# Gated linear attention and a SoLU layer on one core: block transposes placed by four SBUF-to-SBUF DMAs, attention values made as [d, tokens], and the variance of z summed by ScalarE

## The chip, the cores and the metric

The kernel runs on one core of a Trainium2 chip. The metric is device time in microseconds (us) of one execution. Five engines work side by side, each through its own list of instructions in order: PE (TensorE: matmuls, with weight loads shown apart as PEld), DVE (VectorE), ACT (ScalarE), POOL (GpSimd) and SP (SyncE, which here only issues DMAs). SP and ACT can both issue DMAs; in the profile these issues stand as SPq and ACTq.

## The reference, cut to what matters

```python
# attention: q, k, v, a_re, a_im are [B=4, H=8, S=768, D=48]
for t in range(S):                                   # state S_re, S_im: [B, H, D, D]
    new_re = ar * S_re - ai * S_im                   # (ar, ai): the gate of step t, |a| clamped to 0.999
    new_im = ar * S_im + ai * S_re
    S_re, S_im = new_re + k[t] (x) v[t], new_im
    y[:, :, t] = q[t] @ S_re
x = y as [B*S, H*D]                                  # 3072 tokens x 384
# SoLU layer
h = x @ w_in                                         # 384 -> 1024
z = h * softmax(h)
ln = (z - mean(z)) / sqrt(var(z) + 1e-6) * g_ln
out = ln @ w_out                                     # 1024 -> 384
```

Everything is float32 on the chip.

## The kernel before, in words

The sequence is cut into 6 pieces of 128 tokens; with 4 batches that gives 24 chunks `c = 0..23` (`ti, b = divmod(c, 4)`). Two neighbouring chunks form a group `g` (12 of them), for which the gates are prepared together (`prep_steps`). Inside a chunk the recurrence is written as decayed k and q of 96 numbers per head (cosine and sine halves), so that attention is a masked 128x128 product of q and k, plus a product of q with the state of 96x384 that all earlier tokens left (`state[b]`).

The steps of a chunk that the change touches, in the order in which one chunk goes through them:

- `k2`, `q2` (L880, DVE) write the decayed k and q into `f_kq`, tokens on partitions. They are needed with the 96 numbers on partitions and the tokens along the row. `kqb` (L888, DVE) transposes them in blocks of 32x32 into `f_kb`; `kqt0..2` (L896) then bring the blocks to their places in `f_kqT` by 12 DMAs of 32 rows, 6 issued by SP and 6 by ACT. (Chunks 0 and 1 use PE transposes instead.)
- `score0/1` (L937, PE): k times q, in tiles of 32 columns. `mask0` (L941, DVE) masks them into `f_att`, whose rows are key tokens and whose columns are query tokens.
- `values` (L954 and L957, PE): `f_att` as weights, 32 query tokens at a time, times v (48 columns a head), plus `f_kqT` as weights times the state. The result `f_y` has tokens on partitions. `f_vr` is a copy of v of the odd heads with its 32-row blocks in reverse order, since the scores of odd heads lie so.
- `x` (L962, ACT) copies `f_y` from PSUM; `turn_x` (L993, PE) transposes it by three 128x128 products with the identity; `turned_x` (L997, ACT) copies that into `f_xT`.
- `carry` (L970, PE) and `add` (L975 on, DVE) bring the state forward. The PSUM tile of `carry` is the one of `f_y`.
- `up0/1` (L1003, PE), `exp0` (L1008, ACT, with the sum of exponentials), `solu0` (L1011, DVE: h times exp, into `f_z`).
- `blocks` (L1028, DVE) transposes `f_z` in 32x32 blocks into `f_zb`; `away` (L1034) writes them to DRAM by 4 DMAs; `back` (L1039) reads them from DRAM by one DMA as `f_zT`, with the 1024 features on partitions. (Chunks 0, 1, 2 and 23 use PE transposes, `zt` and `zT`.)
- `norm` (L1052 on): mean and variance of z by two `bn_stats` and a `bn_aggr` on DVE, then four small POOL instructions to `f_rs`.
- `down0/1` (L1064, PE), `scale` (L1069, ACT, times `f_rs`), `store` (SP).

The order on every engine is written out by hand: the lists START, EVEN, ODD and END name steps with a chunk number beside each (in EVEN and ODD relative to the chunk `n` of the turn, with `g1`, `g2` for groups), and each step appends its instructions to its engines. EVEN and ODD alternate for n = 2..19, so a period of the loop is a pair of chunks. Each DMA, on SP or ACT, takes the next of 8 semaphores in rotation and waits until the DMA that had it before is done.

Of the kernel before, what the change touches and what calls it, by code (L numbers as in the profile page):

```python
# [19 lines left out]
P = 128  # L20
# [506 lines left out]
phase0:1 load_k:2 last:1 phase1:1 ks1:1 mean:2 qs1:1 mask0:1 convert:12 nearest0:1 nearest1:1 raised:11 part0:1
part1:1 again:0 values:1 clamp:2 cos:1 mean:3 load_vr:3 ends:1 again:1 sin:1 x:1 exp:1 turn_x:1 mean:4
convert:11 again:4 inverse:2 zt0:0 k2:2 mean:5 q2:2 kqb:2 turned_x:1 zT0:0 load_ai:3 kqt0:2 kqt1:2 k2:3 kqt2:2
mean:6 ratio:2 mean:7 tangent:2 q2:3 square:2 secant:2 turn_ends:1 zt1:0 centre:0 fourth:2 centre:7 load_q:2  # L530
up0:1 centre:5 centre:4 up1:1 zT1:0 score0:2 size:2 eps:2 again:2 kqb:3 exp0:1 load_ar:3 tot:1 kqt0:3 centre:1
# [12 lines left out]
square:g2 secant:g2 fourth:g2 ks1:g1 ends:g1 up0:0 load_k:g2 k2:2 q2:2 back:-1 score0:1 zT0:-1 score1:1
load_ai:g3 zt1:-1 turn_ends:g1 size:g2 load_ar:g3 scale:-2 eps:g2 kqb:2 add:0 lnm:g2 tot:g1 mask0:1 zT1:-1 up1:0
kqt0:2 norm:-1 kqt2:2 exp0:0 total1:g2 grow1:g2 inspect:1 total0:g2 grow0:g2 store:-2 decay1:g2 solu0:0 ks0:g2
decay0:g2 store:-3 trig:g2 angle:g2 kqt1:2 blocks:0 on:g2 down0:-1 away:0 down1:-1
# [22 lines left out]
def whole(ctx, tc, flag, q, k, v, a_re, a_im, moe_w_in, moe_w_out, moe_g_ln, out):  # L570
# [634 lines left out]
```

## Time and profile before

| | us |
|---|---|
| median of 3 runs (lowest to highest) | 489.3 (488.15 to 493.79) |
| the profiled execution, its own time | 487.12 |
| the span of its trace, first to last instruction | 484.5 |
| PE busy | 418.7 (86%) |
| DVE busy | 385.8 (80%) |
| ACT busy | 266.6 (55%) |
| POOL busy | 40.8 (8%) |

Some 2.6 us of the profiled execution lie outside the span of its trace. A busy share says how long an engine had work in flight; an engine that is 86% busy can still be the one that everybody waits for in a stage, and what a stage waits for is read from the idle time just ahead of its instructions. The rows that matter are shown in the prediction. PE counts each float32 product as two instructions.

### The profile page before, as it was taken

How to read it: one execution, taken by the hardware profiler on the slowest of the kernel's cores; microseconds unless marked ns; L12 is line 12 of the kernel's file. 1: busy time of each engine (PE TensorE's matmuls, PEld its weight loads, DVE VectorE, ACT ScalarE, POOL GpSimd, SP SyncE). 2: the span in 40 equal slices, each digit the busy share in tenths (PEclk: the TensorE clock that was granted, in tenths of full speed). 3: DMA queues.
4: the chain of work that ended last, by engine and by line, in shares of the span. 5: the costliest groups of instructions: out<-in, count | busy, mean ns of one | idle time of the engine just before them, and what ended most of it. 6: DMA issues, size and time to landing. Idle time of an engine off the chain costs nothing.

```text
span 484.5 us, 14751 instructions
## 1 busy us (share of the span) xinstructions
PE 418.7 (86%) x6244; PEld 282.6 (58%) x6244; DVE 385.8 (80%) x555; ACT 266.6 (55%) x417; POOL 40.8 (8%) x110
## 2 busy tenths in 40 slices
PE   0257977999999988988989998998998997999994
PEld 0035544555676665566666676576675674577762
DVE  5889999798999889789789899689799788482430
ACT  4989967666654743753735654654753743522120
POOL 0000000000001101100110101101001001010010
PEclk9999987999999999999989999999999998999998
DMA  9887957948868769769669759659659758255321
GB/s 246 187 199 216 220 136 178 253 108 175 226 147 200 193 149 212 183 145 210 170 164 225 208 135 216 169 125 222 180 134 214 181 136 224 62 151 145 97 68 41
DMA packets 173419, 82.99 MB, mean 171 GB/s; under 512 B 145312, under 2 KB 158624, under 8 KB 173344
## 3 DMA queue, kind: packets, MB, share of 16 engines
q1 hardware_dynamic: 166864, 72.97, 62.8%
q10 hardware_dynamic: 6480, 8.99, 7.1%
q8 instruction: 51, 0.84, 0.8%
q14 instruction: 24, 0.20, 0.1%
HBM read 49.35 MB, written 15.20 MB: 133 GB/s over the span
## 4 chain that ended last, share of the span: by engine, by line
PE 38%; DMA 19%; DVE 17%; SPq 15%; issue 5%; ACT 4%; ACTq 0%; DVEq 0%
PE f_o L1064 17%; PE f_h L1003 9%; SPq L896 7%; DMA f_zT<-f_zd 6%; DMA f_kqT<-f_kb 5%; SPq L1034 4%; DMA f_zd<-f_zb 3%; DVE f_kb L888 3%; DVE f_kq L880 3%; DMA f_q<-in_q_dram 3%; PE f_score L937 2%; PE f_phase L830 2%; PE f_y L954 2%; DVE f_zb L1028 2%; SPq L648 2%
## 5 line engine op out<-in xcount | busy, mean ns | idle before, releaser
L1064 PE MATMUL f_o<-f_w_out,f_zT 128*128 128x384 f32 x384 | 140.9, 517 | 17.6 <-DMA f_zT<-f_zd 17.1
L1064 PEld LDWEIGHTS f_o<-f_w_out,f_zT 128*128 128x128 f32 x384 | 111.4, 298 | 38.3 <-ACT f_ar L783 12.9
L1003 PE MATMUL f_h<-f_w_in,f_xT 128*128 128x512 f32 x288 | 131.3, 600 | 0.6 <-issue 0.6
L1003 PEld LDWEIGHTS f_h<-f_w_in,f_xT 128*128 128x128 f32 x288 | 52.9, 190 | 56.6 <-issue 53.9
L1008 ACT ACTIVATE f_z<-f_h 128x1024 f32<-128x1024 f32 x24 | 24.5, 1023 | 54.8 <-PE f_h L1003 36.4
L888 DVE STREAM_TRANSPOSE f_kb<-f_kq 128x1536 f32<-128x1536 f32 x22 | 39.1, 1777 | 12.0 <-DMA f_kqT<-f_kb 11.6
L962 ACT COPY f_xn<-f_y 128x384 f32<-128x384 f32 x24 | 11.5, 478 | 64.1 <-PE f_y L957 48.3
L1011 DVE TENSOR_TENSOR f_z<-f_h,f_z 128x1024 f32<-128x1024 f32 x24 | 29.0, 1209 | 19.7 <-ACT f_z L1008 19.7
L1028 DVE STREAM_TRANSPOSE f_zb<-f_z 128x1024 f32<-128x1024 f32 x20 | 41.0, 2052 | 0.4
L937 PEld LDWEIGHTS f_score<-f_kqT 96*32 96x32 f32 x1536 | 29.9, 112 | 17.8 <-issue 16.6
L937 PE MATMUL f_score<-f_kqT 96*32 96x128 f32 (+3 forms) x1536 | 33.6, 239 | 6.6 <-issue 4.3
L776 PE MATMUL f_L<-f_lr,f_mats 128*128 128x384 f32 x48 | 20.4, 553 | 20.8 <-DVE f_lr L771 20.8
L941 DVE TENSOR_TENSOR f_att<-f_score,f_mats 128x1024 f32<-128x1024 f32 x24 | 29.1, 1211 | 6.8 <-PE f_score L937 6.7
L837 DVE SCALAR_TENSOR_TENSOR f_f<-f_f,f_phase 128x384 f32<-128x384 f32 x24 | 13.1, 549 | 26.0 <-ACT f_f L833 26.0
L957 PE MATMUL f_y<-f_state,f_kqT 96*32 96x48 f32 x1280 | 30.8, 206 | 0.0
L1052 DVE BATCH_NORM_STATS2 f_bs<-f_z 128x6 f32<-128x512 f32 x48 | 30.4, 671 | 0.0
L997 ACT COPY f_xT<-f_xt 128x384 f32<-128x384 f32 x24 | 11.4, 476 | 31.4 <-PE f_xt L993 22.6
L957 PEld LDWEIGHTS f_y<-f_state,f_kqT 96*32 96x32 f32 x1280 | 28.4, 110 | 0.2
L776 PEld LDWEIGHTS f_L<-f_lr,f_mats 128*128 128x128 f32 x48 | 9.9, 212 | 29.6 <-DVE f_lr L771 21.4
L954 PE MATMUL f_y<-f_v,f_att 128*32 128x48 f32 x768 | 25.6, 209 | 0.7 <-DVE f_att L941 0.7
L1057 POOL TENSOR_TENSOR f_s<-f_s,f_mv 128x1 f32<-128x1 f32 x24 | 5.0, 208 | 247.1 <-DVE f_mv L1053 247.1
L954 PEld LDWEIGHTS f_y<-f_v,f_att 128*32 128x32 f32 x768 | 16.4, 109 | 14.8 <-issue 11.1
(98 smaller groups left out, 662.1 us busy)
## 6 DMA issues: line engine op xcount, KB each, us to landing
f_zd<-f_zb SPq DMA_DIRECT2D x80, 128.0 KB, 2.7
f_zT<-f_zd SPq DMA_DIRECT2D x20, 512.0 KB, 3.9
f_kqT<-f_kb ACTq DMA_DIRECT2D x132, 64.0 KB, 3.7
f_kqT<-f_kb SPq DMA_DIRECT2D x132, 64.0 KB, 2.0
f_raw<-in_moe_w_out_dram SPq DMA_DIRECT2D x16, 384.0 KB, 4.2
f_raw<-in_moe_w_in_dram SPq DMA_DIRECT2D x12, 512.0 KB, 4.2
f_ar<-in_a_re_dram SPq DMA_DIRECT2D x12, 384.0 KB, 7.9
f_ai<-in_a_im_dram SPq DMA_DIRECT2D x12, 384.0 KB, 5.3
```

Source lines behind the costliest of these rows:

```text
L776: nc.tensor.matmul(out=ps, lhsT=tri, rhs=st["lr"][:, i * DM:(i + 1) * DM], start=True, stop=True)
L888: nc.vector.transpose(out=t, in_=T["kq", c].rearrange("p n h (j f) -> p j (n h) f", f=32))
L896: eng.dma_start(out=T["kqT", c][j * 32:(j + 1) * 32, r], in_=st["kb"][r * 32:(r + 1) * 32, j])
L937: nc.tensor.matmul(out=scores[r0:r0 + 32, x, r:], lhsT=QK[:, r // 32, x], rhs=QK[:, r // 32:, H + x], start=True, stop=True)
L941: nc.vector.tensor_tensor(out=st["att"].rearrange("p (i u) t -> p i u t", u=2), in0=scores.rearrange("p (i u) t -> p i u t", u=2), in1=mat ...
L954: nc.tensor.matmul(out=y[r:r + 32, hs], lhsT=st["att"][:, x, r:r + 32], rhs=rhs, start=True, stop=(ti == 0))
L957: nc.tensor.matmul(out=y[r:r + 32, hs], lhsT=T["kqT", c][:, r // 32, H + x], rhs=state[b][:, hs], start=False, stop=True)
L1003: nc.tensor.matmul(out=st["h"][:, half * 512:(half + 1) * 512], lhsT=st["xT"][:, c * P:(c + 1) * P], rhs=w_in[:, c, half * 512:(half + 1) ...
L1011: nc.vector.tensor_tensor(out=st["z"], in0=st["h"], in1=st["z"], op=OP.mult)
L1028: nc.vector.transpose(out=st["zb"].rearrange("p s t c -> p s c t"), in_=st["z"].rearrange("p (c s f) -> p s c f", s=4, f=32))
L1052: nc.vector.bn_stats(out=bs[:, i], in_=z[:, i * 512:(i + 1) * 512])
L1064: nc.tensor.matmul(out=st["o"], lhsT=st["zT"][:, c] if n in SHORT else st["zT"][:, :, c], rhs=w_out[:, c], start=(c == 0), stop=(c == KF - 1))
```

## The change

Four things change, all in the steps above; the rest of the order stays.

1. `kqb` reads the columns of k and q at a step of 3 elements (12 bytes), so that block element f of block j is feature 3f+j. The 32 rows of a strip and its 3 blocks then follow each other in the order of the 96 features, and one DMA per strip (4 for a chunk, all issued by SP) fills all 96 partitions. `kqt1` and `kqt2` go.
2. `blocks` reads z at a step of 4 elements (16 bytes) in the same manner; `away` takes the blocks from `f_zb` to `f_zT` directly, by 4 DMAs from SBUF to SBUF. `back` and the DRAM tile go.
3. `values` now has v and the state as weights (32 or 16 features) and `f_att` and `f_kqT` as moving data (128 tokens), so that `f_y` comes out with features on partitions; `turned_x` copies it straight into `f_xT`. `x` and `turn_x` go. So that features fill whole strips of 32, `f_vr` and the state get zero columns (odd heads begin 16 columns in), which POOL clears once at the start.
4. `solu0` also sums z; `centred` (POOL) makes minus the mean of it; `spread` (ACT) squares z minus the mean in place, with a sum; `norm` is four POOL instructions on that sum. `bn_stats` and `bn_aggr` go.

```diff
-again:1 values:0 phase0:g1 phase1:g1 qs1:g1 norm:-1 x:0 nearest0:g1 inspect:-1 carry:0 nearest1:g1 qs0:g1
+again:1 values:0 phase0:g1 phase1:g1 qs1:g1 norm:-1 turned_x:0 nearest0:g1 inspect:-1 carry:0 nearest1:g1 qs0:g1
...
-    state = [const.tile([D2, DM], FP, name=f"f_state{b}") for b in range(B)]
+    state = [const.tile([D2, H // 2, P], FP, name=f"f_state{b}") for b in range(B)]
+    odds = [const.tile([P, 2, H // 2, 64], FP, name=f"f_vr{i}") for i in range(3)]
...
-            nc.vector.transpose(out=t, in_=T["kq", c].rearrange("p n h (j f) -> p j (n h) f", f=32))
+            nc.vector.transpose(out=t, in_=T["kq", c].rearrange("p n h (f j) -> p j (n h) f", j=3))
...
-            for r in ((0, 1), (2,), (3,))[i]:
-                for j in range(3):
-                    eng = KQ_ENGINES[i]
-                    eng.dma_start(out=T["kqT", c][j * 32:(j + 1) * 32, r], in_=st["kb"][r * 32:(r + 1) * 32, j])
+            for r in range(4):
+                nc.sync.dma_start(out=T["kqT", c][:, r].rearrange("p x t -> p (x t)"),
+                                  in_=st["kb"][r * 32:(r + 1) * 32].rearrange("p j x t -> p j (x t)"))
...
-            for x in range(H):
-                hs = slice(x * D, (x + 1) * D)
-                rhs = T["vr", g][:, own, x // 2] if x % 2 else V[:, hs]
-                for r in range(0, P, 32):
-                    nc.tensor.matmul(out=y[r:r + 32, hs], lhsT=st["att"][:, x, r:r + 32], rhs=rhs, start=True,
-                                     stop=(ti == 0))
-                for r in range(0, P if ti > 0 else 0, 32):
-                    nc.tensor.matmul(out=y[r:r + 32, hs], lhsT=T["kqT", c][:, r // 32, H + x],
-                                     rhs=state[b][:, hs], start=False, stop=True)
+            queues = [[], [], [], []]
+            for p in range(DM // 32):
+                i, part = divmod(p, 3)
+                todo = []
+                for u in ((0,), (1, 0), (1,))[part]:
+                    x, w = 2 * i + u, 32 if part != 1 or u else 16
+                    o, s0 = 32 * (part - u), 32 * part + 16 * u
+                    vals = T["vr", g][:, own, i, o:o + w] if u else V[:, x * D + o:x * D + o + w]
+                    todo.append((w, vals, st["att"][:, x]))
+                    if ti > 0:
+                        todo.append((w, state[b][:, i, s0:s0 + w], T["kqT", c][:, :, H + x]))
+                for k, (w, lhsT, rhs) in enumerate(todo):
+                    r, c0 = p % 4 * 32, p // 4 * P
+                    queues[p % 4].append(dict(out=y[r:r + w, c0:c0 + P], lhsT=lhsT, rhs=rhs, start=(k == 0),
+                                              stop=(k == len(todo) - 1)))
+            for todo in zip(*queues):
+                for product in todo:
+                    nc.tensor.matmul(**product)
...
-            nc.scalar.copy(out=st["xT"], in_=st["xt"])
+            nc.scalar.copy(out=st["xT"], in_=T["y", n])
...
-            nc.vector.tensor_tensor(out=st["z"], in0=st["h"], in1=st["z"], op=OP.mult)
+            nc.vector.scalar_tensor_tensor(out=st["z"], in0=st["h"], scalar=1.0, in1=st["z"], op0=OP.mult, op1=OP.mult,
+                                           accum_out=st["sum"][:, 0:1])
...
-                                in_=st["z"].rearrange("p (c s f) -> p s c f", s=4, f=32))
+                                in_=st["z"].rearrange("p (c f s) -> p s c f", s=4, f=32))
...
-                nc.sync.dma_start(out=st["zd"][:, :, r].rearrange("s f x -> f s x"),
-                                  in_=st["zb"][r * 32:(r + 1) * 32].rearrange("p s t c -> p s (t c)"))
-        def back():
-            nc.sync.dma_start(out=st["zT"].rearrange("p t c -> p (t c)"),
-                              in_=st["zd"].rearrange("s f r x -> (s f) (r x)"))
+                nc.sync.dma_start(out=st["zT"][:, r].rearrange("p t c -> p (t c)"),
+                                  in_=st["zb"][r * 32:(r + 1) * 32].rearrange("p s t c -> p s (t c)"))
+        def centred():
+            nc.gpsimd.tensor_scalar(out=st["less"], in0=st["sum"][:, 0:1], scalar1=-1.0 / FF, scalar2=None, op0=OP.mult)
+        def spread():
+            nc.scalar.activation(out=st["z"], in_=st["z"], func=AF.Square, bias=st["less"], accum_out=st["sum"][:, 1:2])
...
-                nc.vector.bn_stats(out=bs[:, i], in_=z[:, i * 512:(i + 1) * 512])
-            nc.vector.bn_aggr(out=mv, in_=bs)
...
+    for t in odds + state:
+        nc.gpsimd.memset(t, 0.0)
```

What the list of SP looks like in the loop, from the load of `f_vr` in EVEN to the second `f_kqT` and the stores in ODD; before:

```order
L658 DMA f_vr<-in_v_dram 32x8x48 x4
L648 DMA f_v<-in_v_dram 128x16x48
L896 DMA f_kqT<-f_kb 32x512 x6
L1034 DMA f_zd<-f_zb 32x4x256 x4
L648 DMA f_k<-in_k_dram 128x16x48
L1039 DMA f_zT<-f_zd 128x1024
L648 DMA f_ai<-in_a_im_dram 128x16x48
L648 DMA f_ar<-in_a_re_dram 128x16x48
L896 DMA f_kqT<-f_kb 32x512 x6
L1074 DMA out_dram<-f_ot 128x384 x2
L1034 DMA f_zd<-f_zb 32x4x256 x4
```

and the same stretch of SP's list in the changed kernel:

```order
L659 DMA f_vr_128<-in_v_dram 32x8x48 x4
L649 DMA f_v<-in_v_dram 128x16x48
L895 DMA f_kqT<-f_kb 96x1x512 x4
L1043 DMA f_zT<-f_zb 128x1x256 x4
L649 DMA f_k<-in_k_dram 128x16x48
L649 DMA f_ai<-in_a_im_dram 128x16x48
L649 DMA f_ar<-in_a_re_dram 128x16x48
L895 DMA f_kqT<-f_kb 96x1x512 x4
L1078 DMA out_dram<-f_ot 128x384 x2
L1043 DMA f_zT<-f_zb 128x1x256 x4
```

The blocks of z go to `f_zT` at the place where they went to DRAM, the second transfer is gone, and 6 issues of `f_kqT` have become 4.

ACT's list from the exponential of the even chunk to the last step ahead of the odd chunk's one (lines 754 to 768 prepare the gates of a later group, `f_ar`, `f_u` and `f_x` are their tiles, and `f_ot` is the scaled output of an earlier chunk), before:

```order
L1008 ACTIVATE f_z,f_sums<-f_h 128x1024
L896 DMA f_kqT<-f_kb 32x512 x3
L962 COPY f_xn<-f_y 128x384
L896 DMA f_kqT<-f_kb 32x512 x3
L997 COPY f_xT<-f_xt 128x384
L754 ACTIVATE f_ar<-f_x_2394 128x768
L757 ACTIVATE f_u<-f_ar,f_bias 128x768
L760 ACTIVATE f_ai,f_seen<-f_ar 128x768
L1069 ACTIVATE f_ot<-f_o,f_rs 128x384
L767 ACTIVATE f_u<-f_lr,f_bias 128x768
L768 ACTIVATE f_u<-f_u,f_bias 128x768
L896 DMA f_kqT<-f_kb 32x512 x3
```

and in the changed kernel:

```order
L1014 ACTIVATE f_z,f_sums<-f_h 128x1024
L1003 COPY f_xT<-f_y 128x384
L755 ACTIVATE f_ar<-f_x_2036 128x768
L758 ACTIVATE f_u<-f_ar,f_bias 128x768
L761 ACTIVATE f_ai,f_seen<-f_ar 128x768
L1054 ACTIVATE f_z,f_sum<-f_z,f_less 128x1024
L1073 ACTIVATE f_ot<-f_o,f_rs 128x384
L768 ACTIVATE f_u<-f_lr,f_bias 128x768
L769 ACTIVATE f_u<-f_u,f_bias 128x768
```

ACT's DMA issues and the copy of `f_y` have left the list, and `spread` (L1054) of the even chunk stands ahead of the scaling of an output. The other `spread` of the pair, of the odd chunk, stands in this stretch of ACT's list, ahead of the copy of `f_xT`:

```order
L817 ACTIVATE f_x_2036<-f_x_2036 128x768
L1054 ACTIVATE f_z,f_sum<-f_z,f_less 128x1024
L1003 COPY f_xT<-f_y 128x384
L834 ACTIVATE f_f<-f_phase,f_bias 128x384 x2
```

Ahead of the copy there stood, before, three DMA issues (L896) and the copy of `f_y` (L962).

More of the change, by code (lines that the diff above doesn't have):

```diff
@@ L527 @@
[L527 to L531, printed above, removed]
@@ L539 @@
-sin:g1 exp:g1 mask0:1 inverse:g2 up0:0 up1:0 back:-1 load_vr:g1 exp0:0 k2:2 q2:2 kqb:2 load_v:g2 values:1 kqt0:2
-ratio:g2 down0:-1 kqt2:2 solu0:0 zt0:0 x:1 turn_x:1 blocks:0 carry:1 down1:-1 kqt1:2 tangent:g2 turned_x:1
-away:0
+again:1 values:0 phase0:g1 phase1:g1 qs1:g1 norm:-1 turned_x:0 nearest0:g1 inspect:-1 carry:0 nearest1:g1 qs0:g1
+part0:g1 add:0 load_q:g2 score1:1 last:g1 again:8 scale:-2 part1:g1 score0:1 cos:g1 clamp:g2 sin:g1 exp:g1
+mask0:1 inverse:g2 up0:0 up1:0 load_vr:g1 exp0:0 k2:2 q2:2 kqb:2 load_v:g2 values:1 kqt0:2 ratio:g2 down0:-1
@@ L542 @@
+solu0:0 zt0:0 turned_x:1 blocks:0 carry:1 down1:-1 tangent:g2 away:0
 """
 ODD = """
[L544 to L547, printed above, removed]
+square:g2 secant:g2 fourth:g2 ks1:g1 ends:g1 up0:0 load_k:g2 k2:2 q2:2 score0:1 zT0:-1 score1:1 load_ai:g3
@@ L559 @@
+store:22 scale:23 store:23
 """
@@ L917, in turn_steps @@
             own["kqb"] = blocked
-            own.update({f"kqt{i}": partial(turned, i) for i in range(3)})
+            own["kqt0"] = turned
         return own
@@ L1080, in ffn_steps @@
         else:
-            own.update(blocks=blocks, away=away, back=back)
+            own.update(blocks=blocks, away=away)
         for half in range(2):
```

97 lines of the change are left out of this document (47 added, 50 removed).

## The prediction

> **What bounds the kernel now.** The head of the page and the busy time of three stretches say where PE stands still: the start-up (0 to 80 us), the loop with the first turns of its end (80 to 440), and the last 45 us. The last row below is one pair of chunks of the loop.
>
> ```profile
> span 484.5 us, 14751 instructions
> 0.00:80.00 80.00, 45.58 (x522) 26.77 (x523) 67.68 (x120) 63.02 (x97) 1.66 (x8) 0.97 0.81 201
> 80.00:440.00 360.00, 335.82 (x5387) 228.57 (x5388) 303.67 (x408) 196.02 (x305) 35.56 (x90) 0.98 0.74 176
> 440.00:485.00 45.00, 37.30 (x355) 27.25 (x341) 14.49 (x28) 7.58 (x16) 3.54 (x12) 0.96 0.27 82
> 325.00:361.20 36.20, 33.32 (x553) 23.47 (x552) 30.84 (x42) 20.14 (x32) 3.65 (x9) 1.00 0.76 176
> ```
>
> Columns: stretch, length, then PE, PEld, DVE, ACT and POOL busy, the granted clock, DMA's share. In the loop PE works 335.82 of 360 us, so 24.2 us is all that a better order could give there; a pair takes 36.2 us, of which PE works 33.3, DVE 30.8, ACT 20.1. What PE waits for in that stretch (from the waits of PE; total, times, longest):
>
> ```profile
> PE f_o L1064 <- DMA f_zT<-f_zd: 17.1, 11, 2.7
> PE f_score L937 <- issue: 3.5, 5, 1.1
> PE f_score L937 <- DMA f_kqT<-f_kb: 2.3, 3, 1.0
> ```
>
> So 17.1 of the 24.2 us is the way of z through DRAM. The chain shows that way inside the pair, start and length:
>
> ```profile
> 318.52 2.07 DVE f_zb L1028
> ...
> 326.42 0.45 SPq L1034
> 326.91 2.70 DMA f_zd<-f_zb
> ...
> 329.62 4.66 DMA f_zT<-f_zd
> ...
> 334.42 5.53 PE f_o L1064 x16
> ```
>
> The blocks are ready at 320.6, the last write is issued at 326.4, lands at 329.6, the read lands at 334.3. SP's own list tells why issuing is late (same place one pair later), and ACT's list that it suffers too:
>
> ```profile
> 347.57 3.89 SPq L658 DMA_DIRECT2D f_vr<-in_v_dram  x4
> 355.46 0.39 SPq L648 DMA_DIRECT2D f_v<-in_v_dram  x1
> 356.05 4.68 SPq L896 DMA_DIRECT2D f_kqT<-f_kb  x6
> ```
> ```profile
> 352.12 2.44 ACTq L896 DMA_DIRECT2D f_kqT<-f_kb  x2
> 354.61 0.48 ACT L962 COPY f_xn<-f_y 128x384 f32<-128x384 f32 x1 [2.52 <-DMA f_kqT<-f_kb]
> 356.53 0.48 ACT L997 COPY f_xT<-f_xt 128x384 f32<-128x384 f32 x1 [1.45 <-DMA f_kqT<-f_kb]
> ```
>
> SP stands from 351.5 to 355.5 ahead of a load because the semaphores go round over SP's and ACT's DMAs, and ACT's were issued only at 352 and later. PE is thus the engine that sets the pair, with DVE close behind and the DMA queues making the holes.
>
> **DMAs.** Per pair the 24 transfers of `f_kqT`, 12 on SP and 12 on ACT, become 8 on SP, and the 2 reads of z go; at 4.68 us for six in the row above, SP gains 3 us of issuing and ACT some 8. The bytes of z are moved once, not twice.
>
> ```profile
> f_zd<-f_zb SPq DMA_DIRECT2D x80, 128.0 KB, 2.7
> f_zT<-f_zd SPq DMA_DIRECT2D x20, 512.0 KB, 3.9
> f_kqT<-f_kb SPq DMA_DIRECT2D x132, 64.0 KB, 2.0
> ```
>
> ```profile
> 334.42 5.53 PE L1064 MATMUL f_o<-f_w_out,f_zT 128*128 128x384 f32 x16 [1.87 <-DMA f_zT<-f_zd]
> ```
>
> The new z transfer I price like the write to DRAM, four issues of 0.45 and 2.7 us to landing. On SP it stands behind `f_kqT`, which no longer waits for ACT's issues: with blocks ready at 320.6 it lands near 325.1, 7 us before PE comes to it (332.6 = 334.42 less the idle 1.87). At 4.7 us, as the read took in the chain, it would still be hidden, so no term depends on it. The 17.1 us go, and the 5.8 us on `f_score` partly.
>
> **PE.** Before, `values` of a chunk is 64 products, recorded as 128 passes of 48 columns; now it is 32 products, 64 passes of 128 columns, four strips side by side as before. `score` has 64 passes of 80 columns on average in the same form.
>
> ```profile
> 339.90:341.50 1.60, 1.60 (x130) 1.00 0.45 122
> 344.30:345.55 1.25, 1.25 (x66) 1.00 0.86 211
> ...
> L993 PE MATMUL f_xt<-f_mats,f_xn 128*128 128x128 f32 x72 | 12.5, 282 | 3.3 <-ACT f_xn L962 3.3
> ```
>
> The first row (window of `values`) gives 1.60 us / (32 passes x 48 columns) = 1.04 ns a column and strip, the second (`score`) 1.25 / (16 x 80) = 0.98. New: 16 x 128 = 2048 columns x 0.98 = 2.0 us (1.9 if a pass costs a constant beside its columns, 2.1 at 1.04). So `values` gets 0.4 us longer, although it has half as many instructions. `turn_x` takes 12.5 / 24 = 0.5 us away, or 0.4 without its overlap. PE's work stays as it is: 33.3 us a pair, 0 to +0.2.
>
> **DVE.** Out go two `bn_stats` and a `bn_aggr` a chunk; in come an accumulator read and what strided reading costs the two transposes.
>
> ```profile
> L1028 DVE STREAM_TRANSPOSE f_zb<-f_z 128x1024 f32<-128x1024 f32 x20 | 41.0, 2052 | 0.4
> L888 DVE STREAM_TRANSPOSE f_kb<-f_kq 128x1536 f32<-128x1536 f32 x22 | 39.1, 1777 | 12.0 <-DMA f_kqT<-f_kb 11.6
> L1052 DVE BATCH_NORM_STATS2 f_bs<-f_z 128x6 f32<-128x512 f32 x48 | 30.4, 671 | 0.0
> L795 DVE SCALAR_TENSOR_TENSOR f_k<-f_ai,f_k 128x384 f32<-128x384 f32 x24 | 13.1, 549 | 0.0
> L696 DVE SCALAR_TENSOR_TENSOR f_w_out<-f_raw,f_w_out 128x384 int32<-128x384 int32 x8 | 4.5, 558 | 0.3
> L1053 DVE BATCH_NORM_AGGREGATE f_mv<-f_bs 128x2 f32<-128x12 f32 x24 | 5.0, 209 | 2.2
> L734 DVE DVE_READ_ACCUMULATOR f_ar<-f_ar 128x1 f32 x12 | 0.9, 78 | 0.0
> ```
>
> Out: 2 x 671 + 209 = 1.55 us a chunk. In: 0.08. The transposes: `f_kb` reads and writes in order, 1777 ns for 1536 elements; `f_zb` writes at steps of 32 bytes, 2052 for 1024. If the fixed part is alike (1777 - 1536 x 1.04 = 177), a step of 32 bytes costs 1.83 ns an element where order costs 1.04. Reading at a step of 8 bytes costs nothing (L696, 558 ns, against L795, 549, in order). Reading at 12 and 16 bytes is in no row; bounds: nothing, or what PE's weight load pays for reading `f_zT` at 32 bytes against in order (the two rows of L1064, chunk 22 and chunk 23):
>
> ```profile
> L1064 PEld LDWEIGHTS f_o<-f_w_out,f_zT x16: 312/313/316, 465.1 to 470.1; 128*128 128x128 f32 x16
> ```
> ```profile
> L1064 PEld LDWEIGHTS f_o<-f_w_out,f_zT x16: 186/190/191, 472.2 to 476.8; 128*128 128x128 f32 x16
> ```
>
> that is 123 / 128 = 0.96 ns an element more. For `f_kb` the ends are 0 and 1536 x 0.96 = 1.5 us, for `f_zb` 0 and 1.0 (below nothing is excluded: no access gets shorter). I take +0.6 for `f_kb` (12 bytes lie nearer to 8 than to 32) and 0 for `f_zb`, whose writes, already slow, run beside its reads. A pair: 30.8 - 3.1 + 0.2 + 1.2 = 29.1 us; at the far ends 27.9 to 32.9. Against this change speaks a rule of the Trainium skill, SBUF — State Buffer, section "Door 1: The DMA port swizzle": memory has lines of 16 bytes, and needs two hits on a line for full rate. By it 16 bytes pay fully and 12 bytes mostly (four elements touch three lines); it gives no price, the 8-byte row agrees with it, and with it the sum lies at the far end, the second case below.
>
> **ACT and POOL.** Out: the copy (478 ns) and the 6 issues a chunk; in: `spread`.
>
> ```profile
> L1008 ACT ACTIVATE f_z<-f_h 128x1024 f32<-128x1024 f32 x24 | 24.5, 1023 | 54.8 <-PE f_h L1003 36.4 <-DMA f_k<-in_k_dram 12.1 <-DMA f_kqT<-f_kb 4.0
> L1008 ACT ACTIVATION_READ_ACCUMULATOR f_z<-f_h 128x1 f32 x24 | 4.6, 193 | 0.0
> ```
>
> `spread` is as wide: 1.02 + 0.19, 1.3 us with a margin for its bias. ACT goes from 20.1 to about 21.8 us a pair, far from 33.
>
> ```profile
> 334.95 2.05 DVE L1028 STREAM_TRANSPOSE f_zb<-f_z 128x1024 f32<-128x1024 f32 x1
> ```
>
> Queued behind the odd chunk's `spread`, which waits for `blocks`, is `turned_x`, and behind that `carry` on PE; the transpose ended at 337.0, `spread` then ends at 338.3, and PE ends `values` at 341.5, by 1.9 us sooner at 339.6. Slack 1.3 us: no cost, unless DVE runs late. POOL gets one small instruction a chunk and seven clears at the start, beside 1.66 us of work in 80.
>
> **The sum.** In the loop PE keeps 33.3 to 33.8 us of work a pair and some 0.6 us of holes of the kind `f_score` shows: 34.3 instead of 36.2, over 360 / 36.2 = 9.9 pairs 18.8 us. In the start-up the wait of `f_xt` for the copy (3.3 us in its row) goes, against three longer `f_kb` (+0.6 each) while DVE works 67.7 of 80: -1.5. The last 45 us: PE has no hole until 477, values and `turn_x` balance: 0. Together -20 on the profiled execution's 487.1, 467. The median of the runs is 0.4% above that execution, which gives 469 by medians; I say **468**.
>
> **The rivals.**
>
> *DVE becomes a second bound.* For it speaks the skill's rule, and that DVE keeps a wait in each pair that no step of the change touches:
>
> ```profile
> 327.08 1.78 DVE L888 STREAM_TRANSPOSE f_kb<-f_kq 128x1536 f32<-128x1536 f32 x1 [1.73 <-DMA f_kqT<-f_kb]
> 343.04 0.56 DVE L837 SCALAR_TENSOR_TENSOR f_f<-f_f,f_phase 128x384 f32<-128x384 f32 x1 [2.88 <-ACT f_f L833]
> ```
>
> Of its 5.4 us of idle (36.2 - 30.8) the 1.7 for the DMA go, 3.6 stay. A pair bound by DVE takes 27.9 + 3.6 + X, X being what the transposes add. It decides from X = 2.8 (34.3), and with it the slack ahead of `turned_x` is gone. At X = 4 a pair takes 35.5: -7 in the loop, -1 elsewhere, 479. Range 474 to 483.
>
> *Slower.* The same place, both reads at the weight load's price and reading and writing a block one after the other: X = 2 x (1.5 + 1.0) = 5.0, a pair 36.5, and it decides from X = 4.7. Loop +3, start-up and end another 3 (some 6 longer transposes of 1.5 with half of them hidden, less the wait of `f_xt`): 493; each further ns an element on both adds 5 us a pair, 50 in all. Against it: X is then taken at the top of every bound at once.
>
> *It doesn't do what it says.* The holes of PE come from elsewhere in the loop (a wait that the DMA hid, such as `f_L` for `f_lr`, which DVE makes late in the pair): 2 us a pair come back, 486 to 489.
>
> **How the numbers follow.** Forecast, 457 to 474: 0.60. The low end is PE without any hole in the loop (24.2) and 4 to 6 us out of the start-up. DVE second, 474 to 483: 0.17. No change: 0.11. Slower: 0.12. The range 457 to 488 leaves out the slower case and little more below. Faster or slower than 489.3 by over 1% (4.9 us, about what a measurement here can tell): faster 0.77, within 0.11, slower 0.12.
>
> **What would show it.** Right: no row of `f_o` waiting for `f_zT` in the loop; `values` near 2.0 us a chunk; `f_kb` near 2.4 and `f_zb` near 2.05 us; no waits for `f_kqT` on ACT; a pair near 34.3 us with PE above 97%. Wrong: `f_kb` and `f_zb` at 3 us and more with DVE without idle, or PE waiting for `f_L`, `f_phase` or `turned_x`.

## The result, and the profile after

The changed kernel takes **464.56 us** (median of 4 runs, 463.31 to 464.9); the kernel before took 490.14 (488.15 to 493.79) on the same chip. The ratio is 0.9465, with a 95% interval of 0.9405 to 0.9526. The forecast was 468, in a range of 457 to 488. The profiled execution took 464.73 us.

The head of the page after, and the same kinds of stretch as before (the last row is one pair of chunks):

```profile
span 462.9 us, 11488 instructions
0.00:80.00 80.00, 45.56 (x451) 26.91 (x452) 68.09 (x119) 63.20 (x97) 6.16 (x18) 0.88 0.83 203
80.00:440.00 360.00, 352.09 (x4270) 241.60 (x4270) 297.17 (x376) 215.81 (x336) 45.39 (x118) 0.99 0.70 154
320.00:353.40 33.40, 32.72 (x419) 23.02 (x418) 29.44 (x38) 21.41 (x34) 3.84 (x12) 1.00 0.76 162
```

PE's idle time in the loop fell from 24.2 to 7.9 us. What is left is a new wait (waits of PE after, 80 to 440 us):

```profile
PE f_L L777 <- DVE f_lr L772: 8.2, 9, 2.6
PE f_L L777 <- DVE f_tot L814: 1.8, 1, 1.8
PE f_zt L1028 <- DVE f_z L1018: 0.5, 1, 0.5
```

The longest of them, 2.6 us, lies just ahead of 80 us, so 5.6 us of the first row belong to the loop. No row of `f_o` waiting for `f_zT` and none of `f_score` waiting for `f_kqT` is there. The repeating table loads of ScalarE (L869 before, L870 after) give the period of a pair over seven pairs: 130.58 to 383.29 before, 36.10 us; 33.36 us after.

The sharpest difference is in what SP waits for. Before, between 120 and 390 us:

```profile
SPq L1039 <- DMA f_zd<-f_zb: 14.0, 21, 2.2
SPq L658 <- DMA f_kqT<-f_kb: 11.4, 4, 4.7
SPq L896 <- DMA f_kqT<-f_kb: 9.6, 6, 3.1
SPq L648 <- DMA f_kqT<-f_kb: 7.2, 3, 4.0
...
SPq L1034 <- DVE f_zb L1028: 0.4, 1, 0.4
```

and after, the same stretch:

```profile
SPq L895 <- DVE f_kb L890: 35.7, 13, 7.1
SPq L1043 <- DVE f_zb L1037: 35.0, 17, 7.2
```

Before, all of SP's waits in that stretch come to 70.2 us; 54.2 us of them are for transfers, its own and ScalarE's, and only 0.4 for `f_zb`: when the blocks were ready, SP was mostly still behind. After, no wait for a transfer is listed; SP stands ready and waits for DVE. The costs of the edits, from the groups of the page after and one window of `values`:

```profile
L890 DVE STREAM_TRANSPOSE f_kb<-f_kq 128x1536 f32<-128x1536 f32 x22 | 51.7, 2349 | 0.4
L1037 DVE STREAM_TRANSPOSE f_zb<-f_z 128x1024 f32<-128x1024 f32 x20 | 42.5, 2125 | 0.4
L1054 ACT ACTIVATE f_z<-f_z,f_less 128x1024 f32<-128x1024 f32 x24 | 27.4, 1143 | 13.4 <-PE f_zt L1028 5.6 <-DVE f_zb L1037 5.5 <-DVE f_ok L802 2.3
324.17:326.07 1.90, 1.90 (x65) 1.70 (x64) 0.28 (x1) 0.00 (x0) 1.19 (x3) 1.00 0.87 200
```

Four of the ten executions of one kernel below (y alone), the profiled one among them, were disturbed, so its time is the median of the other six and only PE's waits are read from its trace.

### The profile page after: what moved, and what is told of

The parts are those of the page before. It is cut to its first block, busy times and chain, and to the rows that moved or that the text cites. A ratio compares the mean times of both kernels' runs of the same rounds, so it can differ in the third digit from the quotient of the medians.

```text
span 462.9 us, 11488 instructions
## 1 busy us (share of the span) xinstructions
PE 410.7 (89%) x4764; PEld 277.9 (60%) x4764; DVE 367.7 (79%) x507; ACT 283.4 (61%) x441; POOL 53.0 (11%) x141
## 4 chain that ended last, share of the span: by engine, by line
DVE 43%; PE 38%; issue 7%; ACT 4%; SPq 3%; DMA 3%; DVEq 0%; POOL 0%; ACTq 0%
PE f_o L1068 16%; DVE f_kb L890 9%; PE f_y L969 5%; PE f_h L1009 5%; DVE f_kq L881 5%; DVE f_zb L1037 4%; PE f_L L777 4%; PE f_phase L831 4%; DVE f_z L1018 3%; DVE f_att L941 2%; DVE f_lr L772 2%; DMA f_q<-in_q_dram 2%; DVE f_ai L746 2%; DVE f_lr L765 2%; PE f_d L977 2%
## 5 line engine op out<-in xcount | busy, mean ns | idle before, releaser
L1068 PEld LDWEIGHTS f_o<-f_w_out,f_zT 128*128 128x128 f32 x384 | 111.4, 296 | 16.1 <-issue 4.7
L890 DVE STREAM_TRANSPOSE f_kb<-f_kq 128x1536 f32<-128x1536 f32 x22 | 51.7, 2349 | 0.4
L755 ACT ACTIVATE f_ar<-f_x 128x768 f32<-128x768 f32 x12 | 10.1, 841 | 57.2 <-DVE f_x L752 57.2
L1018 DVE SCALAR_TENSOR_TENSOR f_z<-f_h,f_z 128x1024 f32<-128x1024 f32 x24 | 29.2, 1215 | 19.3 <-ACT f_z L1014 19.3
L969 PE MATMUL f_y<-f_att,f_v 128*32 128x128 f32 (+1 forms) x384 | 37.5, 281 | 0.3 <-DVE f_att L941 0.3
L969 PE MATMUL f_y<-f_att,f_vr 128*32 128x128 f32 x384 | 37.3, 281 | 0.0
L937 PE MATMUL f_score<-f_kqT 96*32 96x96 f32 (+3 forms) x1536 | 33.9, 243 | 2.4 <-DMA f_kqT<-f_kb 2.4
L1054 ACT ACTIVATE f_z<-f_z,f_less 128x1024 f32<-128x1024 f32 x24 | 27.4, 1143 | 13.4 <-PE f_zt L1028 5.6
L941 DVE TENSOR_TENSOR f_att<-f_score,f_mats 128x1024 f32<-128x1024 f32 x24 | 29.1, 1211 | 4.3 <-PE f_score L937 4.1
L969 PE MATMUL f_y<-f_kqT,f_state 96*32 96x128 f32 (+1 forms) x640 | 32.2, 272 | 0.0
L969 PEld LDWEIGHTS f_y<-f_att,f_v 128*32 128x32 f32 (+1 forms) x384 | 20.4, 104 | 14.7 <-DVE f_kq L881 6.1
L1003 ACT COPY f_xT<-f_y 128x384 f32<-128x384 f32 x24 | 11.5, 477 | 27.6 <-PE f_y L969 27.6
```

The costliest lines, as they stand in the source:

```text
L890: nc.vector.transpose(out=t, in_=T["kq", c].rearrange("p n h (f j) -> p j (n h) f", j=3))
L937: nc.tensor.matmul(out=scores[r0:r0 + 32, x, r:], lhsT=QK[:, r // 32, x], rhs=QK[:, r // 32:, H + x], start=True, stop=True)
L941: nc.vector.tensor_tensor(out=st["att"].rearrange("p (i u) t -> p i u t", u=2), in0=scores.rearrange("p (i u) t -> p i u t", u=2), in1=mat ...
L969: nc.tensor.matmul(**product)
L1018: nc.vector.scalar_tensor_tensor(out=st["z"], in0=st["h"], scalar=1.0, in1=st["z"], op0=OP.mult, op1=OP.mult, accum_out=st["sum"][:, 0:1])
L1054: nc.scalar.activation(out=st["z"], in_=st["z"], func=AF.Square, bias=st["less"], accum_out=st["sum"][:, 1:2])
```

## The experiments

The prediction gave one reason for the loop: z's way through DRAM, with the DMAs of `f_kqT` making it later. Twelve kernels take that apart. Names for the four parts: **kq** (4 DMAs, strided `f_kb`), **z** (no DRAM), **y** (values as [d, tokens]) and **var** (variance by ScalarE). "Lag" is the median time from the end of `f_zb` on DVE to SP's first issue of its DMAs, read from the two engines' timelines between 140 and 400 us; "SP issuing" is the summed length of SP's single DMA issues between 120 and 390 us, and "SP waiting" what its own waits list for transfers in the same stretch; a pair is the period over seven pairs as above.

| kernel | median us | ratio to before, 95% | pair us | lag us | SP issuing, of 270 us | SP waiting for transfers |
|---|---|---|---|---|---|---|
| before | 487.8 to 490.7 | 1 | 36.10 | 4.36 | 191.5 | 54.2 |
| the whole change | 464.56 | 0.9465 (0.9405 to 0.9526) | 33.36 | 0.06 | 183.3 | 0 |
| without z | 461.25 | 0.9473 (0.9399 to 0.9547) | 33.26 | 0.03 | 178.7 | 12.8 |
| without kq | 463.48 | 0.9524 (0.9451 to 0.9597) | 32.70 | 1.62 | 213.3 | 16.9 |
| without y | 466.01 | 0.9591 (0.9512 to 0.967) | 33.38 | 0.06 | 190.8 | 0 |
| without var | 461.97 | 0.9497 (0.9422 to 0.9573) | 33.32 | 0.05 | 186.7 | 0 |
| z alone | 458.08 | 0.9374 (0.930 to 0.9448) | 32.96 | 0.40 | 217.8 | 7.5 |
| kq alone | 462.08 | 0.9444 (0.9377 to 0.9511) | 33.22 | 0.03 | 183.9 | 17.2 |
| y alone | 486.32 | 0.9898 (0.9849 to 0.9947) | not read | not read | not read | not read |
| var alone | 495.5 | 1.0107 (1.0064 to 1.0149) | 36.50 | 5.13 | 187.3 | 58.5 |
| kq and z | 464.13 | 0.9495 (0.9456 to 0.9534) | 33.23 | 0.06 | 195.7 | 0 |
| kq, z, `f_lr` sooner | 477.83 | 0.9777 (0.9744 to 0.981) | 34.84 | 0.05 | 177.3 | 0 |
| before, all kqT from SP | 514.41 | 1.0511 (1.0461 to 1.0562) | 39.28 | 6.93 | 235.5 | 13.5 |
| z alone, all kqT from SP | 499.55 | 1.0228 (1.0177 to 1.0279) | 36.96 | 5.54 | 250.9 | 0 |

The last two columns belong together: SP's list was held by issues and by waits for transfers during 246 to 251 of 270 us in the four kernels with a lag over 4 us, and during 177 to 230 us in the other nine that are read. The issues by themselves don't tell the two apart: z alone issues more than the kernel before.

### One part undone

**Without z.** The whole change, but z goes through DRAM again:

```diff
-                nc.sync.dma_start(out=st["zT"][:, r].rearrange("p t c -> p (t c)"),
+                nc.sync.dma_start(out=st["zd"][:, :, r].rearrange("s f x -> f s x"),
...
+        def back():
...
+            nc.sync.dma_start(out=st["zT"].rearrange("p t c -> p (t c)"),
+                              in_=st["zd"].rearrange("s f r x -> (s f) (r x)"))
```

> All of the change but the z path: z goes through DRAM and comes back by one DMA, as before; the four kqT DMAs, the values as [d, tokens] and the variance by ScalarE stay. Theory (the z path was the hole): the 17.1 us in which f_o waited for f_zT come back nearly whole, 464.6 + 13 to 17 = 478 to 482 us, and the trace has a row of PE in f_o waiting for the DMA of f_zT. Rival 1 (the DMAs of kqT, 24 a pair, held SP and the semaphores up, and z through DRAM would be in time once they are gone): 465 to 468 us, with no such row over 2 us. Rival 2 (PE's own work fell and that is the gain): 465 to 468 too.

Measured: 461.25 us. The theory that stood behind the prediction falls here: the trip through DRAM came back and PE waited for it nowhere. Rivals 1 and 2 survive (the time is 4 us below what they gave).

**Without kq.**

```diff
-            nc.vector.transpose(out=t, in_=T["kq", c].rearrange("p n h (f j) -> p j (n h) f", j=3))
+            nc.vector.transpose(out=t, in_=T["kq", c].rearrange("p n h (j f) -> p j (n h) f", f=32))
...
-                nc.sync.dma_start(out=T["kqT", c][:, r].rearrange("p x t -> p (x t)"),
-                                  in_=st["kb"][r * 32:(r + 1) * 32].rearrange("p j x t -> p j (x t)"))
+                for j in range(3):
+                    eng = KQ_ENGINES[i]
+                    eng.dma_start(out=T["kqT", c][j * 32:(j + 1) * 32, r], in_=st["kb"][r * 32:(r + 1) * 32, j])
```

> All of the change but the k and q path: 12 DMAs for the kqT of one chunk, of which 9 from ScalarE's queue, and f_kb from its unstrided reading (1777 ns). Theory: f_zT no longer depends on what these DMAs do, ScalarE has 4 us more a pair against a span of 33.4 with 22.5 busy, DVE gets 0.6 us a chunk back: 463 to 468 us. Rival 1 (the kqT DMAs were the hole): 475 to 485 us, and the trace shows PE waiting for f_kqT, or ScalarE's steps (f_x to f_xT) late by DMA waits.

Measured: 463.48 us, in the theory's range, so rival 1 by itself doesn't hold either. Neither of the two DMA parts is needed beside the other. (As in the kernel before, ScalarE issues six of the twelve DMAs of a chunk, not the nine that were expected.)

**Without y.**

```diff
-                    nc.tensor.matmul(**product)
+                    nc.tensor.matmul(out=y[r:r + 32, hs], lhsT=st["att"][:, x, r:r + 32], rhs=rhs, start=True,
+                                     stop=(ti == 0))
...
+            nc.scalar.copy(out=T["x", c], in_=st["y"])
...
+                nc.tensor.transpose(out=ps[:, c * P:(c + 1) * P], in_=T["x", n][:, c * P:(c + 1) * P], identity=ident)
...
-            nc.scalar.copy(out=st["xT"], in_=T["y", n])
+            nc.scalar.copy(out=st["xT"], in_=st["xt"])
```

> All of the change but the values: 64 products of 64 columns into [tokens, d] again, copied, turned by TensorE and copied again. Theory of the prediction (PE work the same within 0.2 us a pair): 463 to 467 us. Rival 2 (PE's work fell by 1 us a pair since turn_x and the many small products went, as windows of the two traces show, 33.5 to 32.5): 10 pairs by 1 us, 472 to 475 us. The copy of f_xn comes back to ScalarE too, 0.5 us a chunk, which has room.

Measured: 466.01 us, pair 33.38, as the theory had it. Of the 1 us a pair of PE 0.3 came back (PE's work over seven pairs is 32.98 us a pair against 32.67 in the whole change), and the period shows nothing of it, so rival 2 falls.

**Without var.**

```diff
-            nc.scalar.activation(out=st["z"], in_=st["z"], func=AF.Square, bias=st["less"], accum_out=st["sum"][:, 1:2])
+                nc.vector.bn_stats(out=bs[:, i], in_=z[:, i * 512:(i + 1) * 512])
+            nc.vector.bn_aggr(out=mv, in_=bs)
```

> All of the change but the variance: bn_stats and bn_aggr on DVE again, no pass of ScalarE over z. DVE's work rises by 1.55 us a chunk, 3.1 us a pair, from 30.5 to 33.6 us, beside a pair of 33.4. Theory (DVE stands just under PE, so it takes the lead by a little): 466 to 472 us, with waits of PE for DVE in f_L and f_h longer than the 8.2 us of the whole change. Rival 3 (the variance off DVE is what gave the gain, PE having always waited for DVE somewhere): over 478 us. Rival 2 (only PE counts): 464 to 465 us.

Measured: 461.97 us with a pair of 33.32. DVE carried 325.58 of 360 us (297.17 in the whole change), yet PE was not later: in the loop it waited 5.4 us for `f_lr` in place of 5.6. The time is below all three ranges, nearest to rival 2; rival 3 is excluded.

### One part alone

Each single part may go, so the question was which is enough.

**z alone**, against the kernel before (`back` and its places in the order go too):

```diff
-                                in_=st["z"].rearrange("p (c s f) -> p s c f", s=4, f=32))
+                                in_=st["z"].rearrange("p (c f s) -> p s c f", s=4, f=32))
...
-                nc.sync.dma_start(out=st["zd"][:, :, r].rearrange("s f x -> f s x"),
+                nc.sync.dma_start(out=st["zT"][:, r].rearrange("p t c -> p (t c)"),
```

> The kernel before with the z path of the change alone (z goes straight into its place, no trip through DRAM). Undoing this part alone left the time where it was (461 us), so it isn't needed beside the other three; is it enough by itself? Theory A (the trip was the hole, and any one relief closes it): the 17.1 us of waits for f_zT go, PE's work stays as before: 488 minus 15 to 18 = 470 to 473 us. Theory B (the hole was a sign of something else, the DMAs of k and q or late DVE, and moves to another place when the trip goes): 480 to 488 us, with another wait of PE of like size, for f_kqT, f_score or f_L.

**kq alone**, against the kernel before:

```diff
-                    eng.dma_start(out=T["kqT", c][j * 32:(j + 1) * 32, r], in_=st["kb"][r * 32:(r + 1) * 32, j])
+                nc.sync.dma_start(out=T["kqT", c][:, r].rearrange("p x t -> p (x t)"),
+                                  in_=st["kb"][r * 32:(r + 1) * 32].rearrange("p j x t -> p j (x t)"))
```

> The kernel before with the k and q path of the change alone: four DMAs from SP for one kqT in place of twelve from SP and ScalarE; z still through DRAM. Theory A (the trip is late by its own length): the waits for f_zT stay, 483 to 488 us. Theory B (the DMAs of k and q made SP and ScalarE late and with them the trip): the waits for f_zT shrink below 5 us, 468 to 475 us.

Measured: 458.08 and 462.08 us. Each is enough by itself; both together (below) give no more. Both are faster than expected, z alone by 12 us against theory A (470 to 473) and kq alone by 6 us against theory B (468 to 475): these took off the 17.1 us of `f_zT`, but with z alone PE is idle in 4.0 of 360 us, where it was 24.2, so its other waits shrank too. In the run with kq alone z still takes the DRAM, with one visible difference. DVE's, SP's and PE's timeline of one chunk there (start, length, engine):

```profile
302.54 2.06 DVE L1030 STREAM_TRANSPOSE f_zb<-f_z 128x1024 f32<-128x1024 f32 x1
...
299.60 2.91 SPq L893 DMA_DIRECT2D f_kqT<-f_kb  x4
304.63 1.96 SPq L1036 DMA_DIRECT2D f_zd<-f_zb  x4
306.63 0.44 SPq L647 DMA_DIRECT2D f_k<-in_k_dram  x1
308.86 0.34 SPq L1041 DMA_DIRECT2D f_zT<-f_zd  x1
315.06 3.39 PE L1066 MATMUL f_o<-f_w_out,f_zT 128*128 128x384 f32 x10
```

`f_zb` ends at 304.60 and SP issues at 304.63. The read lands at 312.4, 7.8 us after `f_zb`, and PE comes to `f_o` at 315.06. Before, the chunk shown in the prediction had `f_zb` ready at 320.6, and SP's timeline went on:

```profile
319.88 5.36 SPq L896 DMA_DIRECT2D f_kqT<-f_kb  x6
325.34 2.01 SPq L1034 DMA_DIRECT2D f_zd<-f_zb  x4
```

The blocks lay 4.7 us behind six issues of `f_kqT`, the first of which alone took 2.2 us and the others 0.59. The read landed at 334.3, 13.7 us after `f_zb`, and PE had been ready since 332.6, 12.0 us after it; by this sum it would have been in time 4.7 us sooner. What PE still waited for in `f_o` with kq alone (80 to 440 us):

```profile
PE f_o L1066 <- DMA f_zT<-f_zd: 0.3, 1, 0.3
```

So 17.1 became 0.3 us with the trip in place: **the hole was SP's lag in front of a trip that by itself is in time**. A shorter way cures it as well: with z alone, SP keeps 12 issues of `f_kqT` a pair, but loses the read of z with its wait for `f_zd` (14.0 us above); the lag is 0.4 us. ScalarE still issues and waits there (waits of ACT, z alone, 100 to 400 us), and next to nothing of it reaches PE:

```profile
ACT f_z L1012 <- DMA f_kqT<-f_kb: 14.3, 5, 3.0
ACT f_xT L1001 <- DMA f_kqT<-f_kb: 13.8, 6, 3.3
```

**var alone**, against the kernel before:

```diff
-                nc.vector.bn_stats(out=bs[:, i], in_=z[:, i * 512:(i + 1) * 512])
-            nc.vector.bn_aggr(out=mv, in_=bs)
+            nc.scalar.activation(out=st["z"], in_=st["z"], func=AF.Square, bias=st["less"], accum_out=st["sum"][:, 1:2])
```

> The kernel before with the variance by ScalarE alone: DVE is 1.55 us a chunk lighter, ScalarE 1.3 us heavier and still issues the kqT DMAs. Theory A: the waits for f_zT stay, 483 to 488 us. Theory C (DVE came late to f_zb, behind bn_stats): the waits for f_zT shrink below 5 us, 468 to 475 us. If ScalarE is what is short before (its DMA issues), this one is slower than before, 490 to 495 us.

**y alone**, against the kernel before:

```diff
-            nc.scalar.copy(out=st["xT"], in_=st["xt"])
+            nc.scalar.copy(out=st["xT"], in_=T["y", n])
...
+                    nc.tensor.matmul(**product)
```

> The kernel before with the values as [d, tokens] alone: no turn by TensorE, one copy of ScalarE less a chunk. Theory A (trip): the waits for f_zT stay; PE's work falls by up to 1 us a pair, but PE waits in the same places: 478 to 487 us. Theory D (ScalarE's copies, held up between DMA issues, made f_xT and with it z late, so that the trip ended late): the waits for f_zT shrink below 5 us, 466 to 473 us.

Measured: 495.5 us (1.1% slower) and 486.32 us (1.0% faster, at the edge of what can be told). With var alone the waits for `f_zT` stay (80 to 440 us), and ScalarE itself appears:

```profile
PE f_o L1072 <- DMA f_zT<-f_zd: 11.1, 6, 2.2
PE f_o L1072 <- ACT f_ar L787: 4.4, 3, 1.5
```

Theories C and D fall: neither late DVE nor ScalarE's copies were the cause. The time of var alone lies at the top of what was expected if ScalarE is short (490 to 495): more work there does cost, but it isn't the hole at `f_zT`, which z alone closes with all of ScalarE's issues left in. y alone lies in the range of theory A (478 to 487) and far from that of D (466 to 473), and `f_o` still waits 16.1 us for `f_zT` in it.

### SP's queue by itself

**All of kqT from SP**, on the kernel before and on z alone; one line:

```diff
-    KQ_ENGINES = nc.sync, nc.scalar, nc.scalar
+    KQ_ENGINES = nc.sync, nc.sync, nc.sync
```

> The kernel before with one edit: all twelve DMAs of one kqT from SP (before: six from SP, six from ScalarE). z still goes through DRAM. In the trace of before the DMAs of f_zb leave 3 to 5.4 us after f_zb is ready, since SP is busy with six kqT issues that take 5.5 us, 0.9 each, where the four of the kqT path alone take 2.7 us and f_zb's DMAs leave 0.03 us after it. Theory S1 (the number of issues on SP): twelve at 0.5 to 0.9 us are 6 to 11 us, f_zb's DMAs leave later still, the waits for f_zT grow from 2 to some 4 us a chunk: 495 to 515 us. Theory S2 (the six are slow because they wait for semaphores that ScalarE's late DMAs hold): without these the issues take 0.45 us each, the wait for f_zT falls under 1 us a chunk: 468 to 480 us.

> The z path of the change alone, and all twelve DMAs of one kqT from SP. ScalarE loses the waits for f_kqT (14.3, 13.8 and 7.6 us between 100 and 400 us of the run with the z path alone). f_o starts 10.6 us after f_zb there and z needs about 5.3 us (2.6 to issue, 2.7 to landing), so SP may be late by 5 us. Theory S1: SP's twelve issues take 6 to 11 us, which that slack and the wait for f_kb cover: 456 to 462 us. Theory S2: the issues take 5.4 us in all: 455 to 460 us. Rival: kqT comes late for the scores, 465 us or more, with waits of f_score for f_kqT.

Measured: 514.41 and 499.55 us. The first is S1: the timeline of DVE and SP in it shows twelve issues in front of `f_zb`'s:

```profile
185.28 2.05 DVE L1034 STREAM_TRANSPOSE f_zb<-f_z 128x1024 f32<-128x1024 f32 x1
...
181.16 9.31 SPq L898 DMA_DIRECT2D f_kqT<-f_kb  x12
190.57 2.00 SPq L1040 DMA_DIRECT2D f_zd<-f_zb  x4
```

The wait moved in part: PE waited 11.9 us in `f_o` for `f_zT` (17.1 before), and 17.5 us in `f_score` for `f_kqT` (2.3 before). S2's premise was half right: with all of them on SP no wait of SP for `f_kqT` is listed any more, which fits the rounds of the semaphores over two engines as the cause of those waits; but the issues that took their place cost more. The second result is the rival's (465 us or more, with `f_score` waiting for `f_kqT`), and far beyond S1 and S2. SP issued during 250.9 of 270 us, 93%. I had counted only the slack ahead of `f_o` and not the scores, which wait for the same queue (waits of PE, 80 to 440 us):

```profile
PE f_score L938 <- DMA f_kqT<-f_kb: 20.5, 10, 3.7
```

The Trainium skill, DMA: Bandwidth & Descriptors, section "Issuing engines are not separate DMA queues", says that issuing from several engines saves only the sequencer's time for it, usually small beside the transfer. Here it isn't small: an issue of `f_kqT` takes 0.59 us on SP (median) where the transfer takes 2.0 to landing, and one line that gave up the second engine cost 25 us (514.41 against 489.65 on the same chip).

### A better version

**kq and z together** (the two diffs above), and the same with one step of the list ODD moved, since PE's remaining wait in the whole change is `f_L` for `f_lr`, which stands behind the lengthened `f_kb` on DVE:

```diff
-eps:g2 kqb:2 add:0 lnm:g2 tot:g1 mask0:1
+eps:g2 lnm:g2 kqb:2 add:0 tot:g1 mask0:1
```

> The k and q path and the z path of the change together; values and variance as before. Theory (SP's queue was the whole hole, either path empties it, and the other two parts bring nothing): 456 to 462 us, pair 32.8 to 33.3 us. Rival (the parts add up: 28 and 32 us of gain apart): below 445 us. Second rival (DVE, with the 0.6 us of the strided f_kb and bn_stats, takes the lead): 464 to 470 us, PE waiting for f_lr.

> As the run with the k and q path and the z path, and in the odd half of the order the step lnm (f_lr on DVE, which f_L waits for) stands ahead of kqb (f_kb, 2.35 us on DVE). Theory: where PE waits for f_lr (8.2 us in the trace of the whole change, 9 times), that wait goes, and kqT is 0.9 us later, which its place in the order allows: 1 to 6 us less than the run without it, 453 to 459 us. Rival: f_score waits for f_kqT in its place, no gain or up to 4 us more.

Measured: 464.13 and 477.83 us. Both parts together are no better than each (the additive rival, below 445, is excluded), and the time lies 2 us above the theory's range and at the low end of the second rival's, without that rival's sign: PE waited 4.2 us for `f_lr`, 4.0 of it just ahead of 80 us and 0.2 in the loop. The moved step thus had next to nothing to win there; it was chosen by the 8.2 us of the whole change. It made the kernel worse by 14 us, which neither range held. DVE then comes to `f_lr` before ScalarE has made its operand, and everything behind it on DVE is late (waits of DVE and of PE, 80 to 440 us):

```profile
DVE f_lr L770 <- ACT f_u L767: 18.3, 9, 2.5
```
```profile
PE f_L L775 <- DVE f_tot L812: 9.2, 7, 1.6
PE f_L L775 <- DVE f_lr L770: 4.0, 1, 4.0
```

The fastest kernel of the study is z alone: 458.08 us, against 464.56 for the whole change. The two ran on different chips and their intervals overlap (0.930 to 0.9448 and 0.9405 to 0.9526), so that it beats the whole change is likely and not shown. What speaks for it is the period: the kernels with `f_kb` read in order have pairs of 32.70 and 32.96 us, all others with SP free, but for the one with the moved step, 33.22 to 33.38.

## Why the prediction was right, and where it was not

- **The room in the loop** (24.2 us of idle PE, with DVE close behind): right. After, PE is busy in 352.09 of 360 us.
- **"17.1 of the 24.2 us is the way of z through DRAM": the amount was right, the cause was half of it.** The prediction quoted the rows that show SP issuing late, and still put the wait down to the trip, which without the lag is in time. The runs show either of two cures: four DMAs for `f_kqT` with the trip left in (0.3 us of waits), or no trip with all 24 DMAs left in. Since the change holds both, the forecast could not go wrong by it; as a forecast for a kernel without the z part it would have been wrong by some 17 us, as the run without z shows (478 to 482 expected, 461.25 measured).
- **DMAs**: SP's queue was the heart of the matter, and the prediction valued it only as something that makes z land earlier. Over the seven pairs SP's issues fell from 25.8 to 23.3 us a pair (3 us forecast) and ScalarE's from 7.9 to 0 (8 forecast). SP's waits for transfers, which fell from 54.2 to 0 us, were no term of the prediction. The new z transfer takes 0.60 us an issue (0.45 taken) and 2.7 us to landing (2.7 taken). That ScalarE's DMA waits hurt was read into the trace; z alone keeps them and is the fastest.
- **PE, the edit**: `values` 1.90 us a chunk (2.0 predicted). With the part y PE's work is 0.3 us a pair less than without it, where 0 to +0.2 was predicted, and the pair is the same. **PE, the base, was mis-sized**: 33.3 us of work a pair were taken from a kernel with holes. The windows of the seven pairs, before and with z alone, where no instruction of PE was changed, and the groups of `f_o` between 120 and 390 us:

```profile
130.58:383.29 252.71, 233.71 (x3859) 163.60 (x3858) 218.96 (x297) 140.25 (x218) 25.68 (x63) 0.99 0.77 181
L1064 PE MATMUL f_o<-f_w_out,f_zT 128*128 128x384 f32 x239 | 87.3, 514 | 14.4 <-DMA f_zT<-f_zd 14.4
```
```profile
128.10:358.83 230.73, 229.12 (x3858) 163.88 (x3857) 219.52 (x297) 140.31 (x218) 27.62 (x63) 1.00 0.76 167
L1067 PE MATMUL f_o<-f_w_out,f_zT 128*128 128x384 f32 x257 | 90.6, 500 | 0.0
```

  A seventh of PE's time is 33.39 us a pair before, 32.73 with z alone, and 32.67 after the whole change (228.70 in its seven pairs). So 0.4 to 0.7 us a pair of "work" went with the holes (kq alone has 32.89, the whole change without y 32.98). With z alone 0.45 us of it is the 14 ns in each of 32 products of `f_o`: before, the first product behind a hole is recorded with 0.69 us in place of 0.49, and six in a stretch at half the clock (245.5 to 248.9 us) with about 0.85. The idle part went from 2.71 to 0.69 us a pair; what is left is not the kind of hole that `f_score` shows, as the prediction took it, but `f_L` waiting for `f_lr`, one of its own signs of being wrong, at 5.6 us in the loop. The loop gave 22.7 us by the table loads (83.10 to 419.69 before, 83.93 to 397.79 after), where 18.8 were forecast.
- **DVE**: `f_kb` +0.57 (taken +0.6), `f_zb` +0.07 (taken 0), a pair 29.4 (29.1; over the seven pairs 29.93, from 31.28 before). X of the two rivals was 1.3, far from the 2.8 at which DVE would decide. The Trainium skill's rule of 16-byte lines (SBUF — State Buffer, "Door 1: The DMA port swizzle"), by which 16 bytes pay fully and 12 mostly, isn't borne out for these reads: 0.37 ns an element at 12 bytes, 0.07 at 16, the latter beside slow writes, which may hide a part. Still, those 1.1 us a pair on DVE are the likely reason for the 0.3 to 0.7 us by which pairs with strided `f_kb` are longer, and for the 8.2 us of `f_L`: without kq that row is 1.1 us.
- **ACT**: `spread` 1.143 us and 0.19 for its accumulator (1.3 predicted), a pair 21.4 us (21.8). Its cost was hidden here; alone, with the DMA issues still on ScalarE, the same part made the kernel 1.1% slower.
- **Start-up**: -1.5 forecast, +0.8 measured (first table load past 80 us, 83.10 to 83.93). By that mark z alone is 2.5 sooner, kq alone 0.7 sooner and var alone 1.1 later, and the whole change without y is 1.2 sooner than with it. These are single executions, and the granted clock of the first 80 us differs between them (0.97 before, 0.88 after, 0.96 without y, 0.89 with z alone), so which part costs this, if any does, stays open. **End**: 0 forecast; from the last table load to the end of the span 64.8 us before and 65.1 after.

The sum came to -20.3, and the two profiled executions are 22.4 us apart: the loop gave 3.9 more, the start-up 2.3 less, the end 0.3 less, and 0.8 lies outside the spans (2.6 us before, 1.8 after). That the misses in the loop and in the start-up have opposite signs, and partly cancel, is luck.

## What to carry to other kernels

Before a late transfer is blamed on its way, see when its data were ready and when it was issued: a lag there belongs to the issuing engine's queue, and here either of two cuts in that queue cured it. An engine that only issues DMAs is an engine with a budget, so sum its issues and its waits for transfers over a period, and look whether it ever waits for work. When a change has several parts and one hole, each part may be enough and the others may cost a little, so time them alone.

## What the runs showed of the hardware

- An issue between two places in SBUF took SP about the same time for 64 KB (0.589 us median, `f_kqT` in twelve) and for 192 KB (0.605, in four), while landing took 2.0 and 3.4 us. Twelve small for four large thus cost SP 4.7 us more a chunk.
- The granted clock fell to half for some 3.4 us behind stretches in which PE had worked less than half the time. With var alone it did so three times between 85 and 430 us; in the 3.4 us ahead PE was busy for 1.65, 1.16 and 1.36 us. The first of the three, and the stretch ahead of it:

```profile
243.50:246.90 3.40, 1.65 (x90) 1.54 (x79) 3.33 (x5) 1.05 (x3) 1.01 (x3) 1.00 0.80 242
246.90:250.30 3.40, 3.40 (x6) 1.85 (x6) 3.37 (x5) 0.00 (x0) 0.00 (x1) 0.50 0.47 103
```

  The holes beside these three were 1.75, 2.24 and 2.04 us long, and two others, of 2.16 and 2.22 us, had no such drop behind them, so the length of one hole doesn't decide it. PE's idle time in sum doesn't either. With var alone and with z alone and all of kqT from SP, PE was busy equally long (120 to 390 us), and the clock was 0.99 in the first, whose longest wait of PE listed was 2.2 us, and 0.96 in the second, with 3.7 us:

```profile
120.00:390.00 270.00, 250.12 (x4129) 172.71 (x4128) 213.43 (x287) 167.62 (x263) 29.20 (x82) 0.99 0.75 177
```
```profile
120.00:390.00 270.00, 250.25 (x4060) 175.98 (x4058) 231.19 (x313) 148.00 (x231) 23.88 (x69) 0.96 0.66 149
```

  The Trainium skill, TensorE: Matmul & The Clock Gate, "Part 1: The HAM clock gate (the "warmup" mystery)", lets the clock drop after an idle window of about 3.4 us. The length agrees with the stretches at half clock here; a window wholly without work it can't be, since with var alone no hole of the loop was over 2.3 us.
